# Attention and MLP kernel on one core: the first batch's order list is rewritten, and some pieces change engine

## The chip, the cores and the metric

The kernel runs on one core of a Trainium2 chip. The metric is the time of one execution in device microseconds, 579.08 us as the median of 3 runs before the change (578.83 to 579.91).

## The reference

For 8 batches, 12 heads, 448 positions and 64 values a head, the queries and keys are normalised and scaled, a softmax attention is taken, and an MLP with a residual follows.

```python
def rmsnorm(x, g):
    return x / np.sqrt(np.mean(x * x, axis=-1, keepdims=True) + 1e-06) * g
q_n, k_n = rmsnorm(q, g_q), rmsnorm(k, g_k)
scores = np.matmul(q_n, k_n.transpose(0, 1, 3, 2)) / np.sqrt(64)
scores = scores - np.max(scores, axis=-1, keepdims=True)
attn = np.exp(scores)
attn = attn / (np.sum(attn, axis=-1, keepdims=True) + 1e-09)
x = np.matmul(attn, v)            # -> [8, 448, 768], the heads side by side
mu, var = mean and variance of x over its 768 columns
xn = (x - mu) / np.sqrt(var + 1e-06) * g_ln
out = x + np.maximum(xn @ w_ch1, 0.0) @ w_ch2      # 768 -> 3072 -> 768
```

## The kernel before, in words

The heads of a batch are taken in six pairs p. A pair's 448 positions are cut into seven blocks of score rows: six of 128 keys of one head, and a seventh with the 64 left keys of both heads. Pairs are prepared in units. In batch 0, units 0 and 1 hold one pair each (pairs 0 and 1) and units 2 and 3 two pairs each (2, 3 and 4, 5); from batch 1 on every unit holds two pairs. A unit of one pair is a tile of 128x448 values for q and one for k, a unit of two pairs 128x896.

The list ORDER fixes the order of all work of batch 0's attention, and of the first preparation of batch 1. It is written out by hand, and each engine does its own share in the list's order. A later piece never overtakes an earlier one on the same engine. The letters, followed by the unit u or the pair p, are:

- `b` sets up a unit. `a` and `c` square k and q (ScalarE, L260, or GpSimd, L258, for the entries of POOL_SQUARE). `d` and `e` sum the squares of k and q (VectorE, L266). `gq`, `gk` and `g` take the root of the sums by a logarithm and an exponential (ScalarE, L269 and L270).
- `i` multiplies k by the product of the two gains (L280; VectorE for units in DVE_KG, else GpSimd). `j` rounds k to 16 bits (GpSimd for POOL_HI, L286, else ScalarE, L288), and `k` keeps the rest that the rounding lost (L291; GpSimd for POOL_LO, else VectorE). `l` scales q (VectorE, L84). `m` doubles q, so that each position has it twice side by side (L327; GpSimd for POOL_DUP, else VectorE). `z` brings the values into place (GpSimd, L333 and L339).
- `K` and `Q` transpose a pair's k and q by TensorE with an identity matrix (L369 and L372, L383 and L386). The result is copied out of PSUM: kU always by VectorE (L374), qU by ScalarE for pairs in ACT_Q (L389), else by VectorE (L391).
- `Sp.i` is the score block i of pair p (TensorE, L406, and L416 with L417 for the seventh block) and then its exponential E on ScalarE (L422). There are two PSUM banks for scores, so a block waits for the exponential of the block two before. `Vp.i` multiplies E by the values (L459, L461). After `Vp.6` VectorE takes reciprocals and writes the pair's result (L474 to L481); this is called the evacuation of pair p below.
- `T` takes statistics of finished columns (L642), `A` aggregates them (L657), `N` normalises a token tile (L663), `X` transposes it (L699, copied by L703, L705, L707), `R` takes a root. `U` is the first MLP layer for three blocks of 128 hidden values (L946, psU).
- `L` loads a unit's q, k and v by the queue of SP, `W` a third of the first MLP weight by the queue of GpSimd. `H` and `J` are matmuls of the identity by itself into banks that nobody reads (L533, L536).

When the list is done, the MLP of batch 0 begins on TensorE (psH, L719), and from there the attention of batch b+1 is mixed into the MLP of batch b by a planner that works from costs; its calls and their order on TensorE are not touched by the change. Units from 7 on are transposed by DMA, not by TensorE.

Of the kernel before, what the change touches and what calls it, by code (L numbers as in the profile page):

```python
# [27 lines left out]
DVE_KG, POOL_HI, POOL_DUP, ACT_Q = (0, 6), (1, 2, 3, 4, 5, 6, *range(8, 25)), (3, 4, 5, 6), (0, 2, 4, 5)  # L28
POOL_SQUARE, POOL_LO = ((2, 1), (4, 0), (6, 0), (7, 0), (7, 1)), (5, 6)
END_WORK = 44  # L30

# [61 lines left out]
class _Fast:  # L93
# [140 lines left out]
    def pieces(self, u):  # L234

        nc, sh = self.nc, self.sh
        m = UNITS[u][2]
        mh, g = 2 * m, 7 * m
        c = {}
# [86 lines left out]
        def qdup():  # L326
            (nc.gpsimd if u in POOL_DUP else nc.vector).tensor_copy(out=c["qn"][:, :, 1],  # L327
                                                            in_=c["qn"][:, :, 0])
# [35 lines left out]
    def trans_k(self, p):  # L364
# [9 lines left out]
        nc.vector.tensor_copy(out=kT, in_=ps[:, 0:960])  # L374

    def trans_q(self, p):
# [6 lines left out]
        nc.tensor.matmul(ps[:, :, 384:S], qn[:, self.group(p, 6)], sh.id16, is_transpose=True,  # L383
                         start=True, stop=False)
        for i in range(6):
            nc.tensor.matmul(ps[:, i // 3, ts(i % 3, 128)], qn[:, self.group(p, i)], sh.id16,  # L386
                             is_transpose=True, start=False, stop=(i == 5))
# [867 lines left out]
```

## Time and profile before

| | |
|---|---|
| median of 3 runs | 579.08 us (578.83 to 579.91) |
| the profiled execution's own time | 578.86 us |
| its span, from the first to the last instruction | 577.3 us |
| TensorE busy, share of the span | 562.3 us, 97% |
| VectorE busy | 381.6 us, 66% |
| ScalarE busy | 362.7 us, 63% |
| GpSimd busy | 210.3 us, 36% |

The profile is of one execution. A busy time is the sum over an engine's instructions. In a timeline a row has its start and its length in us, the engine, the line of the source, what it writes and reads, the shapes, how many instructions were merged, and in square brackets how long the engine had been idle before it and what ended that. Instructions on one engine can overlap a little at their ends, so that the distance from start to start is some 0.1 us less than the length of a row. GpSimd is called POOL there, VectorE DVE, ScalarE ACT and TensorE PE.

### The profile page before, as it was taken

To read this page: it belongs to the slowest core of one execution; us is meant where nothing else is said; L and a number is where in the kernel's file an instruction comes from. 1 tells how busy PE (TensorE), PEld (TensorE's weight loads), DVE (VectorE), ACT (ScalarE), POOL (GpSimd) and SP (SyncE) were. 2 spreads that over 40 slices of the span, in tenths; PEclk is the share of its full clock that TensorE was granted. 3 is DMA by queue.
4 is the path that set the end of the run, shared out by engine and by line. 5 is a ranking of instruction groups with operands and counts; after the bars stand their busy time and mean duration, and the time that the engine had idled before them with its cause. 6 is when DMAs were issued, how large, how long until landed. Compare 5 with 4: busy or idle time off the path is not lost.

```text
span 577.3 us, 13758 instructions
## 1 busy us (share of the span) xinstructions
PE 562.3 (97%) x5490; PEld 415.1 (72%) x5490; DVE 381.6 (66%) x826; ACT 362.7 (63%) x672; POOL 210.3 (36%) x226
## 2 busy tenths in 40 slices
PE   5788999999999999999999999999999999999998
PEld 4556666687686867777677768777677777878686
DVE  6989577799657586846667586854756733663424
ACT  5998886457674779457675588647777477323130
POOL 5885855404540721554341521654242310020000
DMA  8999999958673956968563797958743490030202
GB/s 215 268 240 221 215 198 169 193 146 123 121 130 85 156 131 140 137 140 115 122 113 48 183 132 131 137 139 143 128 60 65 123 109 1 2 109 1 83 2 58
DMA packets 178329, 72.59 MB, mean 126 GB/s; under 512 B 138212, under 2 KB 173220, under 8 KB 178260
## 3 DMA queue, kind: packets, MB, share of 16 engines
q1 hardware_dynamic: 133876, 52.52, 44.0%
q0 software_dynamic: 43440, 18.52, 24.5%
q8 instruction: 44, 0.72, 0.5%
q10 hardware_dynamic: 944, 0.62, 0.4%
q14 instruction: 25, 0.20, 0.1%
HBM read 52.76 MB, written 11.01 MB: 110 GB/s over the span
## 4 chain that ended last, share of the span: by engine, by line
PE 91%; DVE 4%; ACT 2%; DMA 1%; issue 1%; SPq 0%; POOL 0%; DVEq 0%; ACTq 0%; POOLq 0%
PE psH L799 34%; PE psP L822 30%; PE psS L406 8%; PE oA L459 5%; PE psC L729 4%; PE psH L719 4%; PE oB L461 2%; PE psS L412 2%; ACT E L422 2%; DVE ssq L266 1%; DMA w2s<-in_q_dram 1%; DMA w2s<-in_k_dram 1%; DVE qn L84 0%; PE psW L993 0%; PE tr L372 0%
## 5 line engine op out<-in xcount | busy, mean ns | idle before, releaser
L422 ACT ACTIVATE E<-psS,rr_all 128x448 f16<-128x448 f32 x336 | 204.0, 633 | 48.0 <-PE psS L406 40.4
L799 PE MATMUL psH<-xnT,w 128*128 128x256 f16 (+1 forms) x2016 | 225.7, 261 | 0.0
L799 PEld LDWEIGHTS <-w 128*128 128x128 f16 x2016 | 172.8, 98 | 24.3 <-issue 4.9
L802 ACT ACTIVATE hS<-psH 128x512 f16<-128x512 f32 x150 | 89.8, 599 | 97.3 <-PE psH L799 93.1
L822 PEld LDWEIGHTS <-hS 128*128 128x128 f16 x1080 | 100.0, 98 | 57.3 <-issue 1.1
L822 PE MATMUL psP<-w,hS 128*128 128x384 f16 x672 | 127.0, 326 | 0.0
L406 PE MATMUL psS<-qU,kU 128*128 128x448 f16 x288 | 100.9, 352 | 4.7 <-ACT E L422 2.9
L459 PEld LDWEIGHTS <-E 128*128 128x128 f16 x1008 | 70.3, 98 | 35.7 <-issue 2.8
L280 POOL TENSOR_TENSOR k<-k,gprod 128x896 f32<-128x896 f32 x18 | 38.8, 2157 | 140.0 <-ACT khl L260 95.7
L805 DVE TENSOR_TENSOR hS<-hS 128x512 f16<-128x512 f16 (+1 forms) x119 | 60.0, 511 | 19.3 <-ACT hS L802 17.8
L822 PE MATMUL psP<-w2s,hS 128*128 128x384 f16 (+1 forms) x408 | 69.9, 321 | 0.0
L459 PE MATMUL oA<-v,E 128*128 128x65 f16 x864 | 66.9, 193 | 1.1 <-ACT E L422 0.6
L758 DVE SCALAR_TENSOR_TENSOR x<-psP,rs_all,x 128x384 f32<-128x384 f32 x60 | 36.4, 616 | 42.5 <-PE psP L822 41.8
L461 PE MATMUL oB<-v,E 128*128 128x65 f16 x288 | 52.0, 193 | 0.1
L833 POOL TENSOR_TENSOR x<-x,hS 128x384 f32<-128x384 f32 x21 | 23.5, 1127 | 76.1 <-ACT hS L901 75.5
L474 DVE RECIPROCAL rec_all<-oA 128x6 f32<-128x6 f32 x48 | 9.2, 192 | 53.2 <-PE oA L459 53.1
L217 POOL DMA_DIRECT2D v<-in_v_dram x54 | 41.5, 782 | 4.0 <-PE oB L461 2.7
L406 PEld LDWEIGHTS <-kU 128*128 128x128 f16 x288 | 28.0, 98 | 11.1 <-issue 2.2
L901 ACT ACTIVATE hS<-hS,rs_all 128x384 f32<-128x384 f32 x27 | 14.6, 604 | 33.0 <-DVE hS L805 33.0
L461 PEld LDWEIGHTS <-E 128*128 128x128 f16 x336 | 32.4, 96 | 0.4 <-DVE xl L481 0.3
L84 DVE SCALAR_TENSOR_TENSOR qn<-q,rr_all 128x256 f16<-128x256 f32 (+2 forms) x69 | 24.7, 419 | 7.3 <-ACT rr_all L270 7.2
L266 DVE TENSOR_REDUCE ssq<-khl 128x14 f32<-128x896 f32 (+1 forms) x24 | 25.4, 1060 | 3.7 <-ACT khl L260 3.6
(148 smaller groups left out, 624.0 us busy)
## 6 DMA issues: line engine op xcount, KB each, us to landing
k<-in_k_dram SPq DMA_DIRECT2D x19, 384.0 KB, 4.0
q<-in_q_dram SPq DMA_DIRECT2D x18, 384.0 KB, 3.8
out_dram<-x SPq DMA_DIRECT2D x14, 384.0 KB, 3.1
w<-in_moe_w_ch_dram POOLq DMA_DIRECT2D x3, 1536.0 KB, 14.4
v<-in_v_dram POOLq DMA_DIRECT2D x54, 64.0 KB, 4.5
out_dram<-x POOLq DMA_DIRECT2D x9, 384.0 KB, 2.7
w<-in_moe_w_ch_dram POOLq DMA_DIRECT2D x1, 2304.0 KB, 21.0
w<-in_moe_w_ch_dram POOLq DMA_DIRECT2D x2, 1152.0 KB, 13.9
```

The lines of the kernel that those rows point to most:

```text
L217: nc.gpsimd.dma_start(out[:, :, j, 0:D], main[:, :, j])
L266: nc.vector.tensor_reduce(out=c["ssq"][:, n], in_=c["sq", n], axis=AX.X, op=ALU.add)
L280: (nc.vector if u in DVE_KG else nc.gpsimd).tensor_tensor(out=c["t"][1], in0=c["t"][1], in1=sh.gprod.unsqueeze(1).broadcast_to([128, g, D] ...
L406: nc.tensor.matmul(ps[0][:, 0:S], c["main"][:, ts(i, 128)], c["q"][:, ts(h, S)], start=True, stop=True)
L422: nc.scalar.activation(out=o, in_=x[:, 0:S], func=AFT.Exp, scale=self.units[u][3][:, g:g + 1], bias=EXP_BIAS)
L459: nc.tensor.matmul(oA[:, t, cs], E[:, ts(t, 128)], rhs, start=(i == 0 and t == 0), stop=(i == 6 and t == 2))
L461: nc.tensor.matmul(oB[:, cs], E[:, 320:448], rhs, start=(i == 0), stop=(i == 6))
L758: self.nc.vector.scalar_tensor_tensor(out=x, in0=ps, scalar=self.rs[:, b, t:t + 1], in1=x, op0=ALU.mult, op1=ALU.add)
L799: nc.tensor.matmul(ps[:, i], sh.w1[:, dc, ts(f + i, 128)], self.xnT[:, dc, 256 - N:256], start=(i == 0 and dc == 0), stop=(i == k - 1 and ...
L802: nc.scalar.activation(out=hT[:, f:f + k], in_=ps, func=AFT.Relu)
L805: nc.vector.tensor_tensor(out=out, in0=a, in1=c, op=op)
L822: nc.tensor.matmul(bank[x][:, c], a[:, f], w[:, f, c], start=(start and f == 0), stop=(stop and f == HALF - 1))
```

## The change

The list is written anew: pieces stand in another order, and the identity matmuls (`H`, `J`) are 78 and 22 in place of 76 and 32. The gain product `i` of units 1 and 2 goes from GpSimd to VectorE, and the rounding `j` of unit 1 from GpSimd to ScalarE. The doubling `m` of unit 0 goes from VectorE to GpSimd, that of unit 1 from VectorE to ScalarE. Unit 3's queries are not doubled: each of its two pairs is transposed by 14 matmuls of 64 columns, which write the upper and the lower half of the partitions one after the other, in place of 7. The copy of pair 2's transposed queries goes from ScalarE to VectorE. The squares of q in unit 6 go from GpSimd to ScalarE, after the list's first MLP pieces. A set ACT_K is added and empty. The order of SP's queue stays.

```diff
-DVE_KG, POOL_HI, POOL_DUP, ACT_Q = (0, 6), (1, 2, 3, 4, 5, 6, *range(8, 25)), (3, 4, 5, 6), (0, 2, 4, 5)
-POOL_SQUARE, POOL_LO = ((2, 1), (4, 0), (6, 0), (7, 0), (7, 1)), (5, 6)
+DVE_KG, POOL_HI, POOL_DUP, ACT_Q = (0, 1, 2, 6), (2, 3, 4, 5, 6, *range(8, 25)), (0, 1, 4, 5, 6), (0, 4, 5)
+POOL_SQUARE, POOL_LO = ((2, 1), (4, 0), (7, 0), (7, 1)), (5, 6)
 END_WORK = 44
+ACT_K, ACT_DUP = (), (1,)
+TWICE = (3,)
 ORDER = """
-b0 H12 a0 L4 c0 i0 e0 j0 H24 b1 gq0 d0 k0 l0 a1 m0 K0 G gk0 i1 H10 L5 c1 Q0 d1 j1 S0.0 b2 S0.1
-H5 a2 e1 g1 S0.2 c2 S0.3 k1 l1 z0 d2 e2 m1 K1 S0.4 i2 H16 S0.5 S0.6 Q1 g2 H5 J8 b3 l2 j2 k2 c3
-V0.0 S1.0 z2 S1.1 S1.2 V1.0 J8 a3 m2 H4 V0.1 z3 S1.3 K2 S1.4 V0.2 Q2 V0.3 V0.4 d3 S1.5 V0.5 V0.6
-S2.0 S1.6 V1.1 V1.2 S2.1 e3 W0 i3 K3 V2.0 S2.2 V2.1 S2.3 Q3 j3 T0 S2.4 k3 V1.3 g3 V1.4 S2.5 S2.6
-l3 b4 V1.5 m3 c4 S3.0 S3.1 V2.2 S3.2 K4 a4 V1.6 S3.3 V2.3 S3.4 Q4 d4 V2.4 V2.5 V3.0 V3.1 V3.2
-V2.6 i4 S3.5 j4 J4 S3.6 V3.3 T1 K5 e4 k4 S4.0 W1 S4.1 S4.2 Q5 z4 b5 S4.3 V3.4 V4.0 V3.5 S4.4
-V4.1 V4.2 S4.5 W2 V4.3 S5.0 g4 V3.6 S4.6 S5.1 J4 V5.0 V4.4 G2 S5.2 l4 T3 K6 V4.5 V5.1 V4.6 S5.3
-T4 V5.2 a5 L6 V5.3 S5.4 m4 Q6 i5 S5.5 V5.4 S5.6 V5.5 V5.6 T5 S6.0 S6.1 J4 S6.2 A V6.0 S6.3 V6.1
-N0 N1 S6.4 S6.5 J4 V6.2 X0 V6.3 d5 j5 N2 S6.6 V6.4 X1 z5 Q7 c5 V6.5 R U0 e5 U1 g5 X2 V6.6 M k5
-U2 K7 b6 L7 a6 L8k c6 i6 l5 m5 e6
+b0 a0 L4 c0 b1 H8 i0 e0 H21 H8 j0 k0 gq0 l0 a1 d0 m0 i1 G gk0 K0 d1 c1 L5 Q0 j1 S0.0 e1 H5 g1
+S0.1 b2 a2 z0 c2 S0.2 H34 k1 V0.0 S0.3 i2 l1 e2 m1 d2 J11 S0.4 K1 S0.5 Q1 g2 S0.6 b3 V0.1 c3 H2
+S1.0 j2 S1.1 z2 z3 l2 V0.2 S1.2 a3 V0.3 m2 k2 V1.0 Q2 V0.4 S1.3 d3 V0.5 S1.4 V1.1 K2 V1.2 S1.5
+V0.6 S1.6 S2.0 S2.1 i3 e3 S2.2 j3 K3 k3 W0 S2.3 V2.0 V2.1 Q3 S2.4 V1.3 V2.2 g3 b4 T0 l3 S2.5
+V1.4 V2.3 m3 S2.6 S3.0 S3.1 S3.2 V1.5 a4 V1.6 K4 S3.3 S3.4 V2.4 V2.5 c4 V2.6 Q4 V3.0 V3.1 V3.2
+V3.3 T1 S3.5 z4 d4 S3.6 i4 e4 Q5 W1 K5 S4.0 j4 S4.1 V3.4 k4 S4.2 S4.3 V4.0 V3.5 V4.1 S4.4 W2 b5
+V4.2 V4.3 S4.5 V3.6 V4.4 S5.0 S5.1 J4 T3 g4 V5.0 l4 S4.6 V4.5 V5.1 S5.2 G2 S5.3 K6 V4.6 S5.4
+V5.2 T4 a5 L6 S5.5 m4 Q6 S5.6 V5.3 V5.4 V5.5 V5.6 S6.0 S6.1 i5 S6.2 V6.0 V6.1 T5 S6.3 A J7 N0
+S6.4 S6.5 V6.2 V6.3 X0 N1 d5 j5 V6.4 S6.6 k5 X1 V6.5 N2 c5 z5 Q7 U0 e5 X2 V6.6 U1 R g5 U2 K7 L7
+L8k l5 b6 m5 c6 a6 M e6 i6
 """.split()
@@ def qdup():
+            if u in TWICE:
+                return
+            out, x = c["qn"][:, :, 1], c["qn"][:, :, 0]
+            if u in ACT_DUP:
+                nc.scalar.copy(out=out, in_=x)
+            else:
+                (nc.gpsimd if u in POOL_DUP else nc.vector).tensor_copy(out=out, in_=x)
@@ def trans_q(self, p):
-        nc.tensor.matmul(ps[:, :, 384:S], qn[:, self.group(p, 6)], sh.id16, is_transpose=True,
-                         start=True, stop=False)
-        for i in range(6):
-            nc.tensor.matmul(ps[:, i // 3, ts(i % 3, 128)], qn[:, self.group(p, i)], sh.id16,
-                             is_transpose=True, start=False, stop=(i == 5))
+        for i in (6, *range(6)):
+            o, g = ps[:, :, 384:S] if i == 6 else ps[:, i // 3, ts(i % 3, 128)], self.group(p, i)
+            for r in (slice(0, D), slice(D, 2 * D)) if u in TWICE else (slice(0, 2 * D),):
+                nc.tensor.matmul(o[r], qn[:, g, 0] if u in TWICE else qn[:, g], sh.id16,
+                                 is_transpose=True, start=(i == 6), stop=(i == 5))
```

More of the change, by code (lines that the diff above doesn't have):

```diff
@@ L326, in qdup @@
         def qdup():
-            (nc.gpsimd if u in POOL_DUP else nc.vector).tensor_copy(out=c["qn"][:, :, 1],
-                                                            in_=c["qn"][:, :, 0])
+            if u in TWICE:
[5 more added lines that the diff above has]
+                (nc.gpsimd if u in POOL_DUP else nc.vector).tensor_copy(out=out, in_=x)
         def vmain():
@@ L373, in trans_k @@
                              is_transpose=True, start=False, stop=(i == 5))
-        nc.vector.tensor_copy(out=kT, in_=ps[:, 0:960])
+        if p in ACT_K:
+            nc.scalar.copy(out=kT, in_=ps[:, 0:960])
+        else:
+            nc.vector.tensor_copy(out=kT, in_=ps[:, 0:960])
     def trans_q(self, p):
```

## The prediction

> **What bounds the kernel now.** I read the page's totals first, then the busy times by stretch, then the chain of waits, and the engines' timelines of the first 60 us last. The totals say that TensorE is busy 97% of the span; the stretches say where the other 3% lies.
>
> ```profile
> PE 562.3 (97%) x5490; PEld 415.1 (72%) x5490; DVE 381.6 (66%) x826; ACT 362.7 (63%) x672; POOL 210.3 (36%) x226
> ```
>
> ```profile
> 10.00:20.00 10.00, 6.59 (x78) 4.70 (x77) 9.69 (x12) 7.16 (x14) 8.42 (x9) 1.00 1.10 295
> 20.00:30.00 10.00, 8.27 (x113) 5.72 (x112) 9.16 (x14) 9.75 (x19) 7.48 (x9) 1.00 1.02 236
> 30.00:40.00 10.00, 8.30 (x116) 5.96 (x115) 8.52 (x18) 9.93 (x18) 9.09 (x10) 1.00 1.13 247
> 50.00:60.00 10.00, 9.58 (x127) 7.74 (x125) 9.72 (x20) 7.73 (x18) 6.38 (x6) 1.00 1.12 238
> 60.00:70.00 10.00, 10.00 (x86) 6.44 (x84) 5.54 (x7) 8.28 (x18) 8.87 (x9) 1.00 1.04 192
> 70.00:577.00 507.00, 505.68 (x4840) 374.32 (x4838) 324.11 (x715) 306.61 (x562) 161.08 (x173) 1.00 0.65 111
> ```
>
> From 60 us to the end TensorE misses 1.3 us of 517. In the four earlier stretches shown it idles 7.3 of 40, and there VectorE and ScalarE are near full: 9.69, 9.16, 8.52 and 9.72 of 10 for VectorE, 9.75 and 9.93 for ScalarE. So the span is the time until the MLP begins on TensorE, plus a block of back-to-back matmuls that the change leaves as it is. What the change is worth is how far that beginning moves. The chain that ended last runs, from the evacuation of pair 5 to the last copy of transposed tokens, along VectorE without a pause, and TensorE's last pieces before the MLP hang on that copy:
>
> ```profile
> 39.86 0.20 DVE L474 RECIPROCAL rec_all<-oA 128x6 f32<-128x6 f32 x1 [0.18 <-PE oA L459]
> ...
> 46.54 0.20 DVE L474 RECIPROCAL rec_all<-oA 128x6 f32<-128x6 f32 x1
> ...
> 54.43 0.56 DVE L707 COPY w2s<-tr 128x768 f16<-128x768 f16 x1
> ```
>
> ```profile
> 55.04 1.17 PE L946 MATMUL psU<-w2s,w 128*128 128x128 f16 x18 [0.42 <-DVE w2s L707]
> ```
>
> From 39.86 on no VectorE row up to the copy at 54.43 has an idle time in front of it. The list's end gives VectorE the same instructions in the same order as before (evacuation of pair 5, `T5 A N0 N1 d5 N2 Q7 e5`, the copy of `X2`), so the 8.5 us from 46.54 to 55.04 stay. The question is when VectorE gets to 46.54.
>
> **VectorE's ledger before.** I take each instruction's distance from start to start and subtract what the same form takes where nothing holds it: 0.53 for 128x448 (8.35 to 8.88), 1.00 for 128x896 (28.47 to 29.47), 0.54 for a qU copy (0.62 at 19.17, less the usual overlap), and for a doubling of 448 an estimate of 0.25, half of the 0.48 us that one of 896 lasts.
>
> ```profile
> 8.35 0.62 DVE L291 TENSOR_TENSOR khl<-w2s,khl 128x448 f16<-128x448 f32 x1
> 8.88 0.62 DVE L84 SCALAR_TENSOR_TENSOR qn<-w2s,rr_all 128x448 f16<-128x448 f32 x1
> 9.53 1.11 DVE L327 COPY qn<-qn 128x448 f16<-128x448 f16 x1
> 10.56 0.64 DVE L374 COPY kU<-tr 128x960 f16<-128x960 f16 x1
> 12.45 2.09 DVE L291 TENSOR_TENSOR khl<-w2s,khl 128x448 f16<-128x448 f32 x1 [0.20 <-POOL khl L286]
> 14.46 1.24 DVE L84 SCALAR_TENSOR_TENSOR qn<-w2s,rr_all 128x448 f16<-128x448 f32 x1
> 15.62 1.07 DVE L266 TENSOR_REDUCE ssq<-khl 128x14 f32<-128x896 f32 x1
> 17.61 0.90 DVE L327 COPY qn<-qn 128x448 f16<-128x448 f16 x1
> 18.43 0.63 DVE L374 COPY kU<-tr 128x960 f16<-128x960 f16 x1
> 19.17 0.62 DVE L391 COPY qU<-psQ 128x896 f16<-128x896 f16 x1
> 22.09 0.48 DVE L327 COPY qn<-qn 128x896 f16<-128x896 f16 x1
> 27.93 0.62 DVE L391 COPY qU<-psQ 128x896 f16<-128x896 f16 x1 [0.43 <-PE psQ L386]
> 28.47 1.08 DVE L291 TENSOR_TENSOR khl<-w2s,khl 128x896 f16<-128x896 f32 x1
> 29.47 1.08 DVE L84 SCALAR_TENSOR_TENSOR qn<-w2s,rr_all 128x896 f16<-128x896 f32 x1
> 31.55 0.66 DVE L374 COPY kU<-tr 128x960 f16<-128x960 f16 x1 [0.99 <-PE tr L372]
> ```
>
> ```profile
> 8.94 1.55 POOL L280 TENSOR_TENSOR w2s<-w2s,gprod 128x448 f32<-128x448 f32 x1 [4.42 <-ACT khl L260]
> 12.38 1.68 POOL L258 TENSOR_TENSOR khl<-w2s 128x896 f32<-128x896 f32 x1
> 14.00 1.22 POOL L333 CAST v<-w 128x768 f16<-128x768 f32 x1
> 16.29 2.08 POOL L280 TENSOR_TENSOR w2s<-w2s,gprod 128x896 f32<-128x896 f32 x1
> 30.71 0.93 POOL L327 COPY qn<-qn 128x896 f16<-128x896 f16 x1 [2.91 <-PE oB L461]
> ```
>
> - m0 at 9.53: 1.03 to the next start, 0.78 too long, under GpSimd's i1 (8.94 to 10.49).
> - k1 at 12.45: 2.01, 1.48 too long, under a2 (12.38 to 14.06).
> - l1 at 14.46: 1.16, 0.63 too long, under the cast of values at 14.00.
> - m1 at 17.61: 0.82, 0.57 too long, under i2 (16.29 to 18.37).
> - Waits for TensorE before the copies at 27.93 (0.43) and 31.55 (0.99).
>
> These six make 4.9 us; nine smaller ones of 0.1 to 0.3 us, from l0 at 8.88 (0.12) to the wait at 39.86 (0.18), make 1.9. VectorE lost 6.8 us on its way. What is lost under GpSimd always ends just after the GpSimd instruction does: k1 ends at 14.54, 0.48 after a2.
>
> The Trainium skill (SBUF — State Buffer, Who interferes with whom) puts this down to a pair of ports that the two engines lock for a whole instruction, where two inputs from SBUF are enough for VectorE to need it. By that rule the moved i1 and i2 are new contenders, which speaks against the change; the rival named slower below has its price from rows.
>
> **The change, part by part, on VectorE.** Added: i1 (a form like i0, 0.53), i2 (1.00) and the copy of Q2 (0.54), 2.07 us. Gone: m0 and m1, 0.50 by the estimate. Work: +1.6 us. The losses after, each with its place:
>
> - i0 and e0 stay. d0 now stands behind l0, so k0 waits for ScalarE's j0 (7.41 to 7.99, row below): 0.2.
> - i1 comes at 9.6 and meets m0, now on GpSimd. GpSimd's copy of 448 has no row; one of 896 takes 0.93 (30.71). I take half, 0.5, so 9.3 to 9.8, and i1 loses 0.2. Bounds: 0 and 0.9.
> - a2 follows m0 on GpSimd as soon as its keys have landed. They had by 12.38, when GpSimd came to it; with m0 done at 9.8 it can end between 11.5 and 14.06, and I take 12.2. k1 comes at 12.0: 0.2 lost, where before it was 1.48. Bounds: 0 and 1.5.
> - i2 follows at 12.75, l1 at 13.75. The cast of values, ready by 14.00 in the trace, may slip in between: l1 loses 0.8 of the cast's 1.22. Bounds 0 and 1.7 (both casts).
> - l2 and k2 stand beside the casts z2 and z3 as before: 0.3.
> - d3 now stands before the copy of K2 and waits for a3: 0.3.
> - The two waits at 27.93 and 31.55 (1.4) were for TensorE, which was itself waiting for scores. The copy of K4 now stands behind the evacuation of pair 1. I keep 0.8 for both. Bounds 0 and 1.4.
> - l3 now meets c4, a square on GpSimd of a2's form (1.68): 0.4, bounds 0 and 1.7. The rest 0.3.
>
> Together 3.3 us in place of 6.8. The lower bounds leave what is not held by GpSimd or TensorE, 1.1; the upper ones don't all come at once, since an engine that is held there arrives later at the next meeting, and I bound them by what was lost before, 6.8. Sum: 1.6 + 3.3 - 6.8 = -1.9 us.
>
> **The same by ScalarE**, which is the other full engine.
>
> ```profile
> 7.41 0.58 ACT L288 ACTIVATE khl<-w2s 128x448 f16<-128x448 f32 x1 [0.23 <-DVE w2s L280]
> 11.30 0.91 ACT L389 COPY qU<-psQ 128x896 f16<-128x896 f16 x1 [1.61 <-PE psQ L386]
> 12.64 1.16 ACT L422 ACTIVATE E<-psS,rr_all 128x448 f16<-128x448 f32 x2 [0.44 <-PE psS L406]
> 19.17 0.95 ACT L260 ACTIVATE qn<-w2s 128x896 f32<-128x896 f32 x1 [0.96 <-PE psQ L386]
> 23.73 0.91 ACT L389 COPY qU<-psQ 128x896 f16<-128x896 f16 x1
> ```
>
> Q0's transposes followed m0, which ended at 10.64. l0 is now done at 9.2 instead of 9.5 and m0 at 9.8; c1, moved ahead of the copy of Q0, ends at 10.6. The copy starts at 10.6 instead of 11.30, j1 (0.53) fits behind it while the first score is made, and the first exponential starts at 11.9 instead of 12.64: -0.7. c3 overwrites the tile that Q1 transposes, and waited 0.96 until 19.17 for it, as Q1 waited for m1. m1 now follows l1 by some 0.5 on ScalarE and Q1 is through at about 16.6, ahead of c3: -0.96. The copy of Q2 goes: -0.8, its 0.91 at 23.73 less the overlap. m1 comes: +0.5, as j0's row of 448 is 0.58. Sum -1.9. Both ledgers move by the same amount, so neither engine takes back what the other gives, and I take -1.9.
>
> **What costs nothing, and its cover.** Unit 3's two pairs take 14 transposes more, at most 0.06 us each as later identity matmuls (below), so +0.8, against 10 J fewer and 2 H more, -0.5; TensorE idles 1.7 us between 30 and 40, and without that cover it is +0.3. m3 leaves GpSimd (0.93), and Q4 was not what its copy waited for. GpSimd loses i1, i2 and m3 (1.55, 2.08 and 0.93), so W1 and W2 are issued some 3 us earlier. W0 goes behind i3 and j3 (i2's 2.08 and about 0.9), nearly what leaves ahead of it: it is issued within 2 us of before, near 24.
>
> ```profile
> w<-in_moe_w_ch_dram POOLq DMA_DIRECT2D x3, 1536.0 KB, 14.4
> ```
>
> Such a load took 14.4 us, so it lands by 40, and U reads it near 50. The DMA engines' share is above 1 from 10 us on, so W1 and W2 push the loads of unit 6, which are first squared as the MLP begins: no cost while that cover of some us stands, and what they come late if it is gone. c6 goes from GpSimd to ScalarE in front of a6, 0.85 by the square at 19.17, just as psH begins. TensorE has two more banks to fill before it needs the first one back, and ScalarE is busy 8.28 of 10 from 60 to 70; without that cover the cost is 0.85. M goes from behind the copy of `X2` to the end: nothing.
>
> **The clock.** Identity matmuls take 0.11 us each at first and 0.06 later:
>
> ```profile
> 5.62 2.74 PE L533 MATMUL psW<-id 128*128 128x128 f16 x24
> 9.74 1.05 PE L533 MATMUL psW<-id 128*128 128x128 f16 x10
> 12.63 0.44 PE L533 MATMUL psW<-id 128*128 128x128 f16 x5
> ```
>
> 24 in 2.74 us, then 10 in 1.05, then 5 in 0.44: the step falls in the second row, near 10 us. The ten of 9.74 no longer stand there, and 8 instead of 12 come first; TensorE is as busy from 5.6 to 9.5 as before. I take no change. If the step came one stretch later, at 13.5, Q0's transposes (+0.35), the first scores (0.2 each) and half of the 34 identity matmuls before `V0.0` (0.5) would be late, 0.7 together on the way to the first exponentials: -1.2 and 577.9 us.
>
> The Trainium skill (TensorE: Matmul & The Clock Gate, Part 1 and Part 4) has the clock double after a busy window of some 3.4 us, and says that transposes don't count as busy; by it the seven transposes of K0 are a gap in that window where before ten matmuls followed at once. No run here shows whether it decides, so it is one of the rivals.
>
> **The rivals.**
> - Slower: GpSimd goes on holding VectorE. i1, k1, i2, l1 and later l2, m2, k2 all read two tiles or copy, and each can meet m0, a2 (1.68), the casts of z0 (the first 1.22), z2 and z3. If the losses stay at 6.8 us, the added work comes in full: +1.6, 580.7 us. It decides from 5.2 us of losses. For it: every such meeting in the trace cost VectorE the rest of the GpSimd row. Against it: the two longest rows, i1 (1.55) and i2 (2.08), are gone from GpSimd, and m0 and m1, which lost 1.35, from VectorE.
> - No change: the gain at the first exponential is kept (-0.7), but m1 and c3 on ScalarE wait for l1 and d2, and the waits for TensorE at K3 and K4 come back: losses of about 5, 578.9 us.
> - The late clock above: 577.9 us.
> - More: both waits for TensorE vanish and l1 slips in before the cast: losses of 1.6, -3.6, 575.5 us against the median.
>
> **How the numbers follow.** The profiled execution's 578.86 us is 1.56 over its span and 0.22 under the median of 579.08. 578.86 - 1.9 = 576.96, and against the median 577.2 us. Chances: the forecast, 576.2 to 578.0, 0.5; more gain 0.13; the late clock 0.07; no change 0.13; slower 0.17. A measurement of this kernel tells about 0.2%, 1.16 us, from none. Faster than that: 0.5 + 0.13 and most of the late clock, 0.68; within 0.14, slower 0.18. The range reaches from the largest gain to nearly the slower rival, 575.4 to 580.4; the likeliest case alone is 576.2 to 578.0.
>
> **What would show it.** Right: the last U from 55.04 to about 53.1; the first exponential at 11.9; k1 lasting 0.6 to 0.8 instead of 2.09; no wait on ScalarE before c3; the evacuation of pair 5 starting near 44.6 with VectorE unbroken from there; psH to the end as long as before. Wrong: rows of i1, i2, k1, l1 above 1.2 us, ScalarE waiting for VectorE before m1, identity matmuls at 0.11 us after 12 us, TensorE idle after the MLP has begun, or psH early and the end not.

## The result and the profile after

The changed kernel takes 581.57 us, the median of 22 runs (579.59 to 585.03), against 579.19 us for the kernel before, run beside it (578.67 to 581.60). The ratio is 1.0034, with a 95% interval of 1.0024 to 1.0045: slower by a third of a per cent. (The ratios in this document are not those of the medians, here 1.0041; they lie near those of the means, here 581.46 to 579.51.) The profiled execution took 580.4 us, with a span of 578.8. That is 1.5 us more than the profiled execution of the kernel before, and it is among the faster ones of its kernel.

The busy times by stretch, of the kernel after (columns as before: PE, PEld, DVE, ACT, POOL, then the granted clock, the DMA share and GB/s):

```profile
20.00:30.00 10.00, 7.16 (x99) 4.72 (x96) 9.69 (x13) 9.37 (x18) 8.21 (x8) 1.00 1.03 258
30.00:40.00 10.00, 7.87 (x98) 5.52 (x99) 8.27 (x18) 7.87 (x13) 5.63 (x7) 0.83 1.12 234
60.00:70.00 10.00, 10.00 (x77) 6.27 (x76) 6.05 (x14) 8.89 (x20) 8.00 (x9) 1.00 1.15 217
70.00:577.00 507.00, 506.95 (x4854) 375.32 (x4852) 324.52 (x715) 307.71 (x565) 161.98 (x173) 1.00 0.67 111
```

From 60 us on TensorE is as full as before. The loss lies ahead of that, between 20 and 40 us: TensorE's busy time fell from 8.27 to 7.16 in the first of these stretches, ScalarE's from 9.93 to 7.87 in the second, and in the second the granted clock is 0.83. Finer stretches of the same kernel show where:

```profile
31.00:32.00 1.00, 0.47 (x4) 0.13 (x2) 0.63 (x1) 0.91 (x2) 0.00 (x0) 1.00 1.12 203
32.00:33.00 1.00, 1.00 (x13) 1.00 (x12) 0.25 (x2) 1.00 (x3) 0.58 (x1) 0.50 1.18 218
...
34.00:35.00 1.00, 1.00 (x13) 0.81 (x11) 0.69 (x2) 1.00 (x2) 1.00 (x1) 0.50 1.12 227
35.00:36.00 1.00, 1.00 (x25) 0.82 (x24) 0.85 (x3) 0.26 (x2) 1.00 (x2) 0.80 1.10 225
```

TensorE is given half its clock from 32 to about 35.4 us. What comes ahead of that stands in the timelines of GpSimd, VectorE and TensorE:

```profile
27.48 1.67 POOL L260 TENSOR_TENSOR qn<-hS 128x896 f32<-128x896 f32 x1 [0.51 <-PE psQ L396]
...
27.56 2.54 DVE L293 TENSOR_TENSOR khl<-w2s,khl 128x896 f16<-128x896 f32 x1
30.02 0.61 DVE L401 COPY qU<-psQ 128x896 f16<-128x896 f16 x1
...
30.69 0.55 PE L416 MATMUL psS<-qU,kU 128*128 128x448 f16 x2 [1.86 <-DVE qU L401]
```

`k3` (L293, the rest of unit 3's keys) begins 0.08 us after GpSimd's square `c4` (L260, the queries of unit 4), and takes 2.54 us where the kernel before had 1.08 for it. In the list before, `k3` stood behind `Q3`; the change has put it ahead. So the copy of `Q3` (L401) stands behind it in VectorE's queue, and the first scores of pair 3 need that copy. TensorE stands still for 1.86 us and then runs into the half clock. The beginning of the MLP, from the same kernel's timelines, and behind it that of the kernel before:

```profile
48.20 0.20 DVE L484 RECIPROCAL rec_all<-oA 128x6 f32<-128x6 f32 x1
...
56.07 0.55 DVE L717 COPY w2s<-tr 128x768 f16<-128x768 f16 x1
...
58.17 2.60 PE L729 MATMUL psH<-w2s,w 128*128 128x384 f16 x15
```

```profile
56.44 2.60 PE L719 MATMUL psH<-w2s,w 128*128 128x384 f16 x15
```

The evacuation of pair 5, the copy of `X2` and the MLP's first matmuls come 1.66, 1.64 and 1.73 us later than before (46.54, 54.43 and 56.44).

### The profile page after: what moved, and what is told of

It is laid out like the page before. It is cut to its first block, busy times and chain, and to the rows that moved or that the text cites. A ratio compares the mean times of both kernels' runs of the same rounds, so it can differ in the third digit from the quotient of the medians.

```text
span 578.8 us, 13766 instructions
## 1 busy us (share of the span) xinstructions
PE 564.2 (97%) x5496; PEld 416.5 (72%) x5496; DVE 381.2 (66%) x827; ACT 363.5 (63%) x674; POOL 205.6 (36%) x222
## 4 chain that ended last, share of the span: by engine, by line
PE 91%; DMA 3%; ACT 2%; DVE 1%; SPq 1%; issue 1%; ACTq 0%
PE psH L809 34%; PE psP L832 30%; PE psS L416 8%; PE oA L469 5%; PE psC L739 4%; PE psH L729 4%; PE oB L471 2%; PE psS L422 2%; ACT E L432 1%; DMA k<-in_k_dram 1%; DMA hS<-in_k_dram 1%; DMA w<-in_v_dram 1%; DMA w2s<-in_k_dram 1%; SPq L149 1%; PE tr L379 0%
## 5 line engine op out<-in xcount | busy, mean ns | idle before, releaser
L809 PEld LDWEIGHTS <-w 128*128 128x128 f16 x2016 | 172.8, 98 | 24.1 <-issue 4.8
L843 POOL TENSOR_TENSOR x<-x,hS 128x384 f32<-128x384 f32 x21 | 23.4, 1127 | 76.0 <-ACT hS L911 75.4
```

The costliest lines, as they stand in the source:

```text
L809: nc.tensor.matmul(ps[:, i], sh.w1[:, dc, ts(f + i, 128)], self.xnT[:, dc, 256 - N:256], start=(i == 0 and dc == 0), stop=(i == k - 1 and ...
```

## The experiments

Four theories were tested. T1: the meeting of `c4` and `k3` holds the copy of `Q3`, and the half clock follows. T3: the late full clock at the start is the cost. T4: one of the moved engines costs throughout. T5 and T6 were formed on the way and are told where they come up. Every kernel here computes the whole reference. The times are medians, and each ratio is to the kernel before, run beside it.

**One repair at a time.** In the first text below `k3` is called the query scaling, and its old place is said to be ahead of the copy of `K3`. It is the rest of the keys, L293, and it stood behind `K3` and ahead of `Q3`. The 30 matmuls of the second run are the transposing kind (`J`).

```diff
# e1_k3_behind
-... K3 k3 W0 S2.3 V2.0 V2.1 Q3 S2.4
+... K3 W0 S2.3 V2.0 V2.1 Q3 k3 S2.4
# e2_fill
-V1.4 V2.3 m3 S2.6 S3.0
+V1.4 V2.3 m3 S2.6 J30 S3.0
# e3_warm
-b0 a0 L4 c0 b1 H8 i0 e0 H21 H8 j0 ... G gk0 K0 d1
+b0 H12 a0 L4 c0 b1 i0 e0 H24 j0 ... G gk0 K0 H10 d1
# e4_c4_late
-V2.4 V2.5 c4 V2.6 ... S3.5 z4 d4
+V2.4 V2.5 V2.6 ... S3.5 z4 c4 d4
```

> Edit: k3 (the query scaling on VectorE) put behind the copy of Q3 instead of ahead of K3's copy. Theory T1 (the collision of c4 on GpSimd with k3 on VectorE holds the copy of Q3, TensorE then runs dry before S3.0 and is given half its clock for one window): the copy of Q3 starts near 27.6 us and not 30.0, S3.0 near 28.3 and not 30.7, no half clock at 32 to 35 us, granted clock 1.000, X2's copy near 53.5 to 54.5 us, and the time 1.7 to 3 us below the changed kernel (577.5 to 579.5). Theory T3 (the late start of the full clock is the cost): at most 0.6 us below the changed kernel. Theory T4 (one of the moved engine assignments costs throughout): the same, not below before.

> Edit: 30 identity matmuls on TensorE between S2.6 and S3.0, so that TensorE is busy while it waits for the copy of Q3; the wait itself stays. T2 (the half clock that follows is most of the price, the wait little of it): the copy of Q3 still at about 30.0 us and S3.0 at about 30.7, but granted clock 1.00 between 32 and 36 us, and the time 1.2 to 1.7 us below the changed kernel. T1 (wait and clock together, the wait the larger): 0.3 to 0.9 us below. T3 and T4: no difference over 0.3 us.

> Edit: the identity matmuls of the first 12 us as in the kernel before (12 ahead of a0, 24 ahead of j0, 10 behind K0), the rest of the list as changed. T3 (the late full clock is the cost): full clock from about 10 us, ScalarE's wait before E0.3 (1.21 us) gone, all later stages 1 us or more earlier, and the time 2 us or more below the changed kernel. T1: the first step is as early, but k3 and c4 still meet, S3.0 is still late by 1.5 us or more against the list, and the time is 0 to 1 us below.

> Edit: c4 (GpSimd's square of unit 4) behind z4 instead of behind V2.5, so that it runs some 6 us later and k3 is alone; k3 stays where the changed kernel has it. T1: k3 takes 1.1 us and not 2.5, the copy of Q3 starts near 28.7 us and S3.0 near 29.3, the half clock is gone, and the time is 1.2 to 2.5 us below the changed kernel. If k3's place in the queue and not the collision is the cause: less than 0.5 us. T3 and T4: no difference over 0.3 us, or a loss, since c4 is then later for unit 4.

| kernel | MLP begins (profile) | time | ratio, 95% interval |
|---|---|---|---|
| before | 56.44 | 579.2 | 1 |
| after | 58.17 | 581.57 | 1.0034 (1.0024 to 1.0045) |
| k3 behind Q3 | 55.23 | 581.58 | 1.0038 (1.0017 to 1.0060) |
| identity transposes in the gap | 57.41 | 581.35 | 1.0034 (1.0018 to 1.0050) |
| start as before | 57.73 | 581.22 | 1.0034 (1.0022 to 1.0045) |
| c4 later | 54.31 | 584.28 | 1.0082 (1.0067 to 1.0097) |

The first and the last missed by far, and in one way. T1 was right on the stage it speaks of: with `k3` behind `Q3` the copy started at 26.65 us, with `c4` out of the way `k3` took 1.08 us and the copy started at 27.23, the half clock at 32 us was gone in both, and the MLP began 2.9 and 3.9 us earlier than in the changed kernel. The time did not follow. The kernel that began the MLP first was the slowest of all. With `c4` later, in VectorE's timeline:

```profile
26.23 1.08 DVE L293 TENSOR_TENSOR khl<-w2s,khl 128x896 f16<-128x896 f32 x1
27.23 0.62 DVE L401 COPY qU<-psQ 128x896 f16<-128x896 f16 x1
```

The timelines of ScalarE and TensorE, with `k3` behind `Q3`, tell why the time did not follow:

```profile
59.59 0.95 ACT L262 ACTIVATE qn<-q 128x896 f32<-128x896 f32 x1 [3.91 <-DMA q<-in_q_dram]
...
57.86 0.65 PE L729 MATMUL psH<-w2s,w 128*128 128x384 f16 x3
61.81 0.49 PE L729 MATMUL psH<-w2s,w 128*128 128x384 f16 x2 [3.30 <-ACT hS L732]
```

and the same with `c4` later:

```profile
60.66 0.95 ACT L262 ACTIVATE qn<-q 128x896 f32<-128x896 f32 x1 [5.89 <-DMA q<-in_q_dram]
...
62.88 1.11 PE L729 MATMUL psH<-w2s,w 128*128 128x384 f16 x3 [5.29 <-ACT hS L732]
```

`c6`, the square of unit 6's queries, which the change moved to ScalarE, waits for the transfer of these queries. (The expectations and the names of the runs call it `a6`; in the list `a6` is the square of the keys, which follows it.) The evacuations of the MLP's first blocks stand behind it in ScalarE's queue, and TensorE stops for 3.3 and 5.3 us, with a second half clock after it (a granted clock of 0.83 and of 0.66 between 60 and 70 us). What the head, the stretch ahead of the MLP, had gained went into waiting.

The identity transposes did take the half clock at 32 us away in the profile (1.00 from 28 to 36 us), and 6 of 11 runs had a granted clock of 1.000 where none of the changed kernel's 22 had. The MLP began 0.76 us earlier and again met the late queries, with 1.3 us of waiting. This execution had a half clock of its own at the start (a granted clock of 0.53 from 12 to 14 us and 0.62 from 14 to 16), and its copy of `Q3` started at 30.32, 0.30 us later than the changed kernel's. From that copy to the MLP it took 1.06 us less. So the half clock at 32 us is worth some 1.1 us, and the wait ahead of it the rest of the 2.9 to 3.9 that came from taking the meeting apart, less what the next paragraph finds for the start.

With the start as before the 34 identity matmuls ahead of `V0.0` took 2.06 us and not 2.73, ScalarE's wait at 16.6 us fell from 1.21 to 0.41, the MLP began 0.44 us earlier, and the time did not change: T3 falls as the main cause. From TensorE's timeline, the changed kernel and then the one with the start as before:

```profile
13.54 2.73 PE L543 MATMUL psW<-id 128*128 128x128 f16 x34
```

```profile
13.39 2.06 PE L543 MATMUL psW<-id 128*128 128x128 f16 x34
```

But the late full clock does not come from the change's start alone. Of the 13 profiles here of kernels with that start, ten show 2.06 us for this row and three 2.73 to 3.19; the four with the start as before all show 2.06. The changed kernel's profile was one of the three. Two relatives with its list up to 35 us and the early clock (`c6` on GpSimd, and `W1` later, both below) began the MLP at 57.76 and 57.46, so 0.4 to 0.7 of the 1.73 us by which it was late are likely this execution's start.

**Is it ScalarE's queue?** T5 says that `c6` on ScalarE is the fault, since the kernel before had it on GpSimd.

```diff
# e11_a6_back (the changed kernel); the same line with k3 behind Q3 in e12_k3_a6,
# with k3 and the start as before in e13_k3_warm_a6, with c4 later in e14_c4_a6
-POOL_SQUARE, POOL_LO = ((2, 1), (4, 0), (7, 0), (7, 1)), (5, 6)
+POOL_SQUARE, POOL_LO = ((2, 1), (4, 0), (6, 0), (7, 0), (7, 1)), (5, 6)
```

> Edit: the changed kernel with a6 (the square of unit 6's queries) on GpSimd again instead of ScalarE; nothing else. Theory T5 (on ScalarE a6 waits for the transfer of unit 6's queries, and the first evacuations of the MLP wait behind it, so that TensorE stops at 58 to 62 us in the runs where this transfer is late): the half clock at 32 to 35 us stays (granted clock 0.997), but no run has a second dip (0.994), and the median falls from 581.6 to between 580.0 and 580.6 us. If only the collision of k3 with c4 counts (T1): median 581.0 to 582 us.

> Edit: k3 behind the copy of Q3, and a6 on GpSimd. T1 and T5 together: MLP starts on TensorE at about 55.2 us as with k3 moved alone (58.2 in the changed kernel), the wait of 3.3 us for ScalarE behind it is gone, granted clock 1.000, and the time is 577.5 us (576.8 to 578.3), below before. If the transfer of unit 6's queries gates the MLP in another way too (through unit 6's own work on TensorE): 579 to 581 us.

> Edit: as the one before, and the identity matmuls of the first 12 us as in the kernel before (12 ahead of a0, 24 ahead of j0, 10 behind K0). T3 in its small form (the late full clock costs what it delayed, 0.4 us as the start of the MLP moved between the changed kernel and the one with these matmuls alone, 58.17 and 57.73): 577.1 us (576.4 to 578.0), 0.4 below the one before. If ScalarE and VectorE take the delay up: no difference over 0.3 us between the two.

> Edit: c4 on GpSimd behind z4 instead of behind V2.5 (k3 stays ahead of K3's copy), and a6 on GpSimd. T5: c4 moved alone began the MLP at 54.3 us and lost it in a wait of 5.3 us behind a6; with a6 on GpSimd this wait is gone, granted clock 1.000, and the time is 576.6 us (576.0 to 578.0), the lowest of the four. If the earlier issue of the weights' transfers makes unit 6's data late for TensorE itself: 579 to 582 us, with a wait of PE behind the MLP's first strip.

Measured: 582.45 us (1.0050, 1.0035 to 1.0065), 583.39 (1.0064, 1.0052 to 1.0076), 581.31 (1.0045, 1.0027 to 1.0063) and 583.67 (1.0070, 1.0056 to 1.0084). T5 falls: all four stay slower than the kernel before; against the same lists with `c6` on ScalarE the first two are 0.9 and 1.8 us slower and the last is 0.6 us faster. ScalarE no longer waits for the transfer, and the wait goes on along another way. From the timelines of GpSimd, VectorE and TensorE with `k3` behind `Q3` and `c6` on GpSimd:

```profile
61.19 1.68 POOL L260 TENSOR_TENSOR qn<-q 128x896 f32<-128x896 f32 x1 [1.94 <-DMA q<-in_q_dram]
...
62.91 1.09 DVE L268 TENSOR_REDUCE ssq<-qn 128x14 f32<-128x896 f32 x1 [4.04 <-POOL qn L260]
...
66.61 0.63 PE L396 MATMUL tr<-id,qn 128*128 128x128 f16 x7 [3.53 <-DVE kU L384]
```

GpSimd waits for the same transfer, VectorE's sum waits for GpSimd, the copy of transposed keys stands behind that sum, and TensorE stops all the same. Whichever engine takes `c6`, its queue is held until the queries are there. What counts is when they land.

**When do the queries land?** Unit 6's queries go through SP's queue. The three thirds of the first MLP weight, `W0` to `W2`, go through GpSimd's. The queue rows of the profile for 40 to 56 us, where both have work, of the kernel with `k3` behind `Q3`:

```profile
q0 software_dynamic: 1354, 2.73, 89.9%
q1 hardware_dynamic: 1352, 0.74, 21.8%
```

The first is GpSimd's queue, the second SP's: as many packets from the one as from the other, but of 2.0 KB against 0.55 KB, so SP gets a fifth of the bytes. The Trainium skill (DMA: Bandwidth & Descriptors, Queues, rings and completion order) has each DMA engine go round the queues that have work and take one packet from each; this trace agrees, 1354 packets beside 1352. SP's queue gets the DMA engines nearly to itself only between two weights. The same rows for 36 to 40 us, of the kernel before and then of the one with `k3` behind `Q3`:

```profile
q1 hardware_dynamic: 1753, 1.01, 93.8%
q0 software_dynamic: 80, 0.14, 18.5%
```

```profile
q0 software_dynamic: 332, 0.65, 85.9%
q1 hardware_dynamic: 373, 0.24, 25.1%
```

Before, `W0` was all but through and `W1`, issued at 36.26 us, had hardly begun: SP's queue moved 1.01 MB in 4 us. With `k3` moved, `W0` was issued 2.3 us later (26.12) and was still under way; `W1`, issued at 34.05 us, followed it without a break, and SP's queue moved 0.24 MB. The transfers of unit 6's queries landed 6.6 to 8.9 us after their issue in the first kernel and 19.1 to 23.4 us in the second:

```profile
DMA to landing us min/median/max: 6.6/7.2/8.9
```

```profile
DMA to landing us min/median/max: 19.1/23.3/23.4
```

T6: `W1`, issued before SP's queue has passed unit 6's queries on, makes them late. The bytes that the core had moved by the time `W1` was issued (mean GB/s of that stretch by its length) sort the profiles made so far:

| kernel (profile) | W1 issued, us | MB moved by then | queries land after issue, us (median) |
|---|---|---|---|
| before | 36.26 | 8.59 | 7.2 |
| after | 35.94 | 8.66 | 12.5 |
| start as before | 35.78 | 8.48 | 22.1 |
| identity transposes | 36.13 | 8.42 | 23.3 |
| after, c6 on GpSimd | 35.66 | 8.31 | 23.2 |
| k3 behind Q3 | 34.05 | 8.00 | 23.3 |
| c4 later | 34.69 | 8.01 | 24.1 |

(The three left out lie at 7.99 to 8.10 MB and 22.9 to 23.9 us.) Below 8.5 MB the queries took at least 9 us longer than in any profile above it. The line is drawn afterwards, between 8.48 and 8.59. The changed kernel's profile stands just above, the relative with only `c6` elsewhere just below. In the changed kernel the queries were issued 5 us earlier than before (30.4 and 35.3), so that its 12.5 us end at the same time on the clock: the last landed at 46.1 us, and at 46.2 before. Four runs put T6 to the test:

```diff
# e15_w0_early (with k3 behind Q3)
-S2.0 S2.1 i3 e3 S2.2 j3 K3 W0 S2.3
+S2.0 S2.1 W0 i3 e3 S2.2 j3 K3 S2.3
# e16_w1_late (with k3 behind Q3) and e18_after_w1_late (the changed kernel)
-Q5 W1 K5 ... S4.4 W2 b5 ... m4 Q6 S5.6 ... i5 S6.2
+Q5 K5 ... S4.4 b5 ... m4 W1 Q6 S5.6 ... i5 W2 S6.2
# e17_before_w0_late (the kernel before)
-S2.1 e3 W0 i3 K3 V2.0
+S2.1 e3 i3 W0 K3 V2.0
```

> Edit: k3 behind the copy of Q3, and W0 (the first third of the MLP's weights) ahead of i3 on GpSimd, so that it is issued near 23 us as in the kernel before (23.8) and not at 26.1. Theory T6 (the three weight transfers run without a break once W1 is issued before W0 has landed; the loads of units 6 and on, on SP's queue, then get the small share, unit 6's queries land 23 us after their issue instead of 7 to 9, and whichever engine squares them stops the MLP): with 11 us between W0 and W1 instead of 8 the queries land within 14 us, the MLP starts near 55.3 us without a later wait, granted clock 1.000, 577.5 us (577 to 579). If W0's place does not matter: as with k3 moved alone, 581 to 582 us.

> Edit: k3 behind the copy of Q3, and W1 and W2 later on GpSimd (behind m4 and behind i5, near 43 and 46 us instead of 34 and 37); W0 stays where the changed kernel has it. T6: W0 has landed near 41 us, unit 6's queries land by 45 us, no wait behind the MLP's first strips, granted clock 1.000, MLP from 55.2 us, 577.5 us (577.0 to 578.3). If the queries are late for another reason: 581 to 582 us as with k3 moved alone. If W1 and W2 then land too late for the MLP: a wait of TensorE's psH matmuls for DMA near 70 us.

> Edit: the kernel BEFORE with W0 behind i3 instead of ahead of it (issued 2.1 us later, near 25.9 us), nothing else. T6: the weights' transfers close up, unit 6's queries land 17 to 24 us after their issue, GpSimd's a6 waits for them at 57 us and VectorE's and TensorE's queues behind it, 580.5 to 583 us. If the changed kernel's loss comes from its own list and engines alone: 579.2 us, no difference over 0.3.

> Edit: the changed kernel with only W1 and W2 later (as two above; k3 stays ahead of K3's copy). T1 and T6: the half clock at 32 to 35 us stays (0.997 in all runs, none 0.994), the MLP starts near 58.2 us, and nothing stops it: 580.0 us (579.6 to 580.6), the low end of the changed kernel's runs. If the weights do not matter: 581.6 us.

`W1` later with `k3` behind `Q3`: 578.08 us, 0.9976 (0.9964 to 0.9988), faster than the kernel before. In its profile the queries landed in 3.2 to 6.9 us, the MLP began at 55.95 us, and nothing stopped it:

```profile
55.95 2.60 PE L729 MATMUL psH<-w2s,w 128*128 128x384 f16 x15
58.58 1.14 PE L729 MATMUL psH<-w2s,w 128*128 128x384 f16 x6
```

`W1` later alone: 580.48 us, 1.0031 (1.0011 to 1.0052), with the queries in time (4.6 to 8.3 us), the half clock of 0.83 between 30 and 40 us still there, and the MLP from 57.46 us. Nine of its 11 runs lie between 579.66 and 580.85, near where the expectation had them; two at 584.8 and 585.4 are not explained.

The two runs on `W0` were misses. Issued at 22.65 us it held SP's queue earlier: unit 6's queries were only issued from 45.5 us on, the last landed at 59.3, and the time was 582.12 us (1.0042, 1.0023 to 1.0061). And the kernel before with `W0` 2.4 us later took 579.65 us, 1.0012 (0.9999 to 1.0025): there the queries still landed in 7.0 to 10.7 us, with 8.71 MB moved when `W1` was issued at 36.77. So the distance between `W0` and `W1`, by which the expectations went, does not decide alone: it was 11.0 us in the first of these, with late queries, and 9.9 in the changed kernel, with queries in time. (The second, at 10.6, agrees with either view.) How far SP's queue has come when `W1` is issued fits all of them; that it is the only condition is not shown.

The four kernels without and with each repair:

| | W1 where the change has it | W1 and W2 later |
|---|---|---|
| k3 ahead of Q3 | 1.0034 | 1.0031 |
| k3 behind Q3 | 1.0038 | 0.9976 |

By these ratios neither repair does anything alone, and the two together take 0.6%. With `k3` repaired the head runs into the late queries; with the weights repaired the head is still late. The ratio of the kernel with only the weights later (1.0031) is held up by its two unexplained runs. By the medians that kernel is 1.1 us slower than the one before, and the changed kernel 2.4, so that later weights alone may well be worth some 1.3 us in most executions. T4 falls with it: with all its moved engines the change is faster than the kernel before once these two are out of the way.

**What the rest is worth.** The last six runs ask whether the weights' place would have helped the kernel before, what the start, the meeting and the double transposition are worth once both repairs are in, and whether the weights were moved too far.

```diff
# e19_before_w1_late (the kernel before)
-S4.0 W1 S4.1 ... S4.5 W2 V4.3 ... m4 Q6 i5 S5.5
+S4.0 S4.1 ... S4.5 V4.3 ... m4 W1 Q6 i5 W2 S5.5
# e20_w1_warm: e16_w1_late with the start of e3_warm
# e21_w1_c4: e18_after_w1_late with c4 as in e4_c4_late
# e22_w1_no_twice: e16_w1_late with
-... (0, 1, 4, 5, 6), (0, 4, 5)
+... (0, 1, 3, 4, 5, 6), (0, 4, 5)
-TWICE = (3,)
+TWICE = ()
# e23_mid_c4_warm: e20_w1_warm with c4 as in e4_c4_late, and, as in e24_mid_no_twice
# (e22_w1_no_twice), the weights earlier:
-S5.2 G2 S5.3 ... m4 W1 Q6 S5.6 ... i5 W2 S6.2
+S5.2 G2 W1 S5.3 ... m4 W2 Q6 S5.6 ... i5 S6.2
```

> Edit: the kernel BEFORE with W1 and W2 moved on GpSimd behind m4 and behind i5, nothing else. Theory T6 (the place of the weights matters only where unit 6's queries would be late): the kernel before already has these queries in time in its profile, so 579.1 us (578.7 to 579.5), at most 0.3 us below before; then the changed kernel with the same two moves and k3 behind Q3 (578.08) is a gain of the change itself. If the weights' place is worth as much here: 578.0 us.

> Edit: the kernel with k3 behind Q3's copy and W1 and W2 later (578.08 us), and with it the identity matmuls of the first 12 us as in the kernel before. T3 in its small form: 0.4 us less, 577.6 us (577.1 to 578.1). If the late clock is hidden: 578.1 us. If the clock's delay holds the first stage by all of its 1.2 us wait of ScalarE: 576.9 us.

> Edit: the changed kernel with W1 and W2 later, and c4 on GpSimd behind z4 so that it no longer runs beside k3; k3 stays ahead of Q3's copy. T1 (the meeting counts, not k3's place): k3 takes 1.1 us, the half clock at 32 us is gone, the MLP starts near 54.8 us as with c4 moved alone (54.3), and with unit 6's queries in time the kernel takes 577.2 us (576.6 to 578.2). If k3's place counts: 580 us or more. If c4's late start holds unit 4: 578.5 to 580 us.

> Edit: the kernel with k3 behind Q3's copy and W1 and W2 later (578.08 us), and with it unit 3's queries doubled by GpSimd again (0.93 us of a copy) instead of transposed twice by TensorE. If GpSimd is in time at this place (it idled 2 to 3 us near 30 us), doubling by GpSimd costs nothing and saves 14 transposes of some 0.07 us: 577.6 to 578.1 us. If GpSimd's copy comes late for the fourth transposition, as my prediction had it for the kernel before: 578.6 to 579.2 us.

> Edit: the changed kernel with k3 behind Q3's copy, c4 behind z4, the identity matmuls of the first 12 us as before, and W1 and W2 only 3 us earlier than in the runs above (behind the scaling of the gains and behind m4, near 39 to 41 and 42 us). If the weights were too late there: unit 6's queries still land by 46 us, the MLP starts at 54.0 us, no wait of psC for the weights near 107 us, 576.3 us (575.8 to 577.2). If the transfers bound the whole stretch up to 110 us whatever the order: 578 us or more, with such a wait or a late load in it.

> Edit: as the kernel without the double transposition (579.68 us), with W1 and W2 3 us earlier (behind the scaling of the gains and behind m4). If that kernel lost by the late last weights alone: the MLP starts at 54.5 us as there, the wait of 1.6 us is gone and 577.0 to 577.8 us, so that the double transposition is worth nothing here. If the double transposition is what it lacks: 579 us or more.

| kernel | MLP begins (profile) | wait for the last weights | time | ratio, 95% interval |
|---|---|---|---|---|
| before, W1 later | 56.51 | none | 579.49 | 1.0006 (0.9990 to 1.0021) |
| k3, W1 later | 55.95 | none | 578.08 | 0.9976 (0.9964 to 0.9988) |
| the same, start as before | 54.86 | none | 577.96 | 0.9973 (0.9962 to 0.9985) |
| c4 later, W1 later | 54.33 | 1.8 | 578.46 | 0.9986 (0.9973 to 0.9999) |
| k3, W1 later, not transposed twice | 54.51 | 1.6 | 579.68 | 1.0013 (0.9998 to 1.0028) |
| all repairs, W1 some 4 us earlier | 54.42 | none | 578.28 | 0.9982 (0.9965 to 1.0000) |
| not transposed twice, W1 some 4 us earlier | 54.43 | 1.0 | 578.88 | 0.9985 (0.9973 to 0.9997) |

- The weights' place is worth nothing to the kernel before. The gain of 0.24% with both repairs is therefore the change's own.
- The start as before is worth 0.1 us, within the noise: T3 falls in its small form too. What a late clock at the start costs in the time is not shown by it, since both profiles have the early one (2.06 us for the 34 identity matmuls).
- The meeting counts more than the place of `k3`: with `c4` out of the way and `k3` still ahead of `Q3`, `k3` took 1.09 us, and the MLP began at 54.33; behind `Q3` but still beside `c4` it took 3.01, and the MLP began at 55.95.
- Beginning at 54.3 us brings no further gain. The next transfer is late instead. From the timeline of TensorE, with `c4` and `W1` later:

```profile
107.51 1.78 PE L739 MATMUL psC<-w,hS 128*128 128x384 f16 x10 [1.79 <-DMA w<-in_moe_w_ch_dram]
```

- Without the double transposition GpSimd's doubling `m3` comes ahead of `c4`, so `k3` is alone there too: 1.08 us, against 3.01 in the kernel with both repairs.
- With the weights some 4 us earlier and unit 3 not transposed twice, that wait fell from 1.6 to 1.0 us and the time by 0.8 us. The double transposition itself: 578.88 without it and 578.28 with it at the same place of the weights (the second also with the other start and `c4` later), intervals that overlap. Whether it is worth anything stays open.
- All repairs together did not beat the two: 578.28 us, from 576.35 to 581.78. Its best run is the fastest of the study, but its runs spread over 5 us, those of the two repairs over 3. What sets a run's place in this spread is open.

The kernel with the lowest median is the changed one with `k3` behind `Q3`, `W1` and `W2` later and the start as before: 577.96 us, 0.27% below the kernel before (0.15 to 0.38%).

## Why the prediction was wrong

The forecast was 577.2 us within 575.4 to 580.4, and faster. The kernel is slower, 581.57 us, above the range.

**The ledgers.** Their sum, -1.9 us at the MLP's beginning, would have been 54.5. (VectorE's losses after, as listed, add up to 3.5 and not to 3.3, which makes it -1.7 and 54.7.) In the changed kernel it came out as 58.17, and with the one meeting of `c4` and `k3` taken out as 54.31 to 54.33. With `c4` later the evacuation of pair 5 started at 44.35, where the forecast had 44.6. So the work, and the meetings that the ledger had listed, came out rightly in the sum. The places agree too, in the timelines of VectorE and ScalarE of the kernel after:

```profile
12.39 0.63 DVE L293 TENSOR_TENSOR khl<-w2s,khl 128x448 f16<-128x448 f32 x1 [0.34 <-ACT khl L290]
...
13.94 1.25 DVE L86 SCALAR_TENSOR_TENSOR qn<-w2s,rr_all 128x448 f16<-128x448 f32 x1
...
19.56 0.94 ACT L262 ACTIVATE qn<-w2s 128x896 f32<-128x896 f32 x1
```

`k1` fell from 2.09 to 0.63 us, `l1` still meets a cast and takes 1.25, and `c3` no longer waits. The first exponential started at 12.51 and not 11.9. With the same start it came at 11.75 to 12.81 in the other profiles, 11.97 in the one with only `W1` and `W2` later, so 11.9 was within reach.

**First failed step: "l3 now meets c4 ...: 0.4, bounds 0 and 1.7".** `c4` was put beside the wrong instruction. It follows `W0` on GpSimd at 27.5 us, where VectorE begins `k3`, which the change had moved ahead of `Q3`, and the price was 1.46 us (2.54 less 1.08). By its size that is within the bounds. But behind `k3` stands the copy of `Q3`, for which TensorE and ScalarE's exponentials wait, and with them the clock. Between kernels with the early clock and late weights the repair was worth 1.5 us at the MLP's beginning with `k3` behind `Q3` but still beside `c4`, and 3.1 with `c4` later (57.46 against 55.95 and 54.33). A meeting was priced as lost VectorE time; it is priced by what is queued behind it.

**Second failed step: "I take no change" for the clock, and no drop after the start at all.** At the start the late clock came in the changed kernel's profile as the rival had it: 34 identity matmuls in 2.73 us from 13.54, a step near 14 us. The rival's 0.7 us is near the 0.4 to 0.7 at the MLP's beginning found above. But the step varies between executions of this start, and no run shows its price in the time. The drop that cost was another, at 32 us, behind TensorE's own wait, some 1.1 us. Neither the forecast nor a rival had it.

**Third failed step: "W1 and W2 push the loads of unit 6 ...: no cost while that cover of some us stands".** The place was right and so was the condition, and the cover was taken to stand without its size being worked out. The issue times were wrong: `W1` came 0.3 us earlier than before and not some 3 (35.94 and 36.26), `W2` 1.0 us later, and `W0` 2.3 us later (26.09 and 23.78). In the profiled execution the cover just held: there the loss is 1.5 us by its own time, all of it ahead of the MLP. The median's loss is 2.4 us. That the difference comes from runs where the queries came late is likely, since the same list with `c6` elsewhere shows them late at 8.31 MB, since later weights alone brought the median from 581.57 to 580.48, and since six of the changed kernel's 22 runs have a granted clock of 0.994, where the profile with one half clock has 0.997. No profile shows such a run of the changed kernel itself. What the runs do show is that with the ledger's gain in hand this cover is gone: -2.9 us at the MLP's beginning gave 0.0 us of time.

**With it fell the frame: "a block of back-to-back matmuls that the change leaves as it is".** Where nothing is late the block does take as long as before: 520.9 us from the MLP's beginning to the span's end in the kernel before (577.3 less 56.44), 520.6 in the changed kernel, 520.5 with `k3`, the weights and the start repaired (575.4 less 54.86). It is a block only as long as the transfers have time to be ahead of it. The rival named slower (580.7) had the sign and, in the profile, the size: it had +1.6 us, and the evacuation of pair 5 came 1.66 later. Its mechanism, GpSimd holding VectorE, came true at one place that it did not list, `k3` under `c4`, and through what stood behind it. Of the losses under GpSimd that the ledger had named, those of `m0`, `k1` and `m1` went and that of `l1` stayed (1.25 us for 0.62). That this rival came so near in the time is in part luck, since the median holds the late queries too.

## What to carry to other kernels

Before a gain ahead of a long full stretch is booked, look up for each transfer that the stretch needs when it lands and how much later it may: an engine set free issues its own bulk transfers earlier, and those take the packets of the small ones that are needed first. Price a meeting of two engines by what stands behind the held instruction in its queue, not by its length. When a repair shifts the stage as expected and the time not at all, there is a second wait just behind; repair both before either is called useless.

## What the runs showed of the hardware

- Two DMA queues with work share by packets, not by bytes: 1354 and 1352 packets, 2.73 and 0.74 MB, between 40 and 56 us.
- Landing times jump rather than drift: 5 to 13 us after issue (medians) with 8.59 MB or more moved when `W1` is issued, 22 to 24 us with 8.48 MB or less. The one kernel off this line, with `W0` early, had 12.2 us because the issue itself came 10 us late. That the sharing makes the jump is argued, not measured apart.
- The clock is halved for some 3.4 us after much less than 3.4 us of standing still: waits of 1.86 and 0.53 us between 28.8 and 31.8 us were enough in the changed kernel, while the wait of 1.79 us at 107 us in an otherwise full stretch left the clock at 1.00.
- The Trainium skill (TensorE: Matmul & The Clock Gate, Part 4) says that transposes don't count as busy in the same way for this gate. With 30 identity transposes in the gap at 28.8 us, and nothing else added, 6 of 11 runs kept a granted clock of 1.000, where without them none of 22 did, and two of 11 with the same head and `W1` later. These runs speak against the page's rule, as far as one change in one place can.
- `k3` beside a GpSimd square of 1.67 to 1.70 us took 0.94 to 1.95 us longer (2.02 to 3.03 against 1.08), in four profiles more than the square itself lasted (3.01 to 3.03).
